# Conv 0 of an S4D block: VectorE's order fixed from the last doublings to the second norm, its spectra in four tiles, and the constants for U loaded twice

## The chip, the cores and the metric

The kernel runs on one core of one Trainium2 chip. A core has five engines with a queue each: TensorE (PE, with its weight loads PEld), VectorE (DVE), ScalarE (ACT), GpSimd (POOL) and SyncE (SP, which only issues DMAs). Each engine works through its own list of instructions in the order in which the program put them there, and waits on semaphores where an instruction needs something that another engine or a DMA has not finished. The metric is device time in microseconds (us) for one execution, the median of several runs.

## The reference

An adaLN-conditioned block on x of shape (1, 2048, 576), all float32: a layer norm with shift and scale, a long convolution whose kernel comes from an S4D state-space model with 128 states a channel, a gated residual, a second norm, and a dense ReLU layer 576 to 4608 to 576 with a gated residual.

```python
dt = exp(log_dt); A = -exp(log_A_real) + 1j * A_imag; C = (C_real + 1j * C_imag) * dt[:, None]
K = 2 * einsum("dn,dnl->dl", C, exp((A * dt[:, None])[:, :, None] * arange(L))).real
y = irfft(rfft(u_t, 2 * L) * rfft(K, 2 * L))[..., :L] + u * D_skip        # per channel
sa, ca, ga, sb, cb, gb = split(silu(c) @ w_mod, 6)
h = layernorm(x) * (1 + ca) + sa;  x = x + ga * conv(h)
h = layernorm(x) * (1 + cb) + sb;  x = x + gb * (relu(h @ w1) @ w2)
```

## The kernel before, in words

The 2048 positions are cut into four blocks of 512. Block s of the convolution needs kernel taps of blocks 0 to s, so the dense layer (FFN) of block 0 can start once block 0 has been convolved; everything of blocks 1 to 3 is then spread between the FFN's matmuls by `step`, which draws from generators. This study is about the front, which nothing covers: taps of block 0, convolution of block 0, second norm, first FFN matmul (`hps`).

**Taps of block 0** (`KGen.first`). The 576 channels come in six groups g of 96. `values` makes two factors by exp, sin and cos; `doubling` (L210) grows factor W1 from 1 to 16 powers in four steps, each two products `t`, `T` and two sums; in the last step the sums are POOL's. `multiply` has TensorE form the taps `kps`, `rows` copies them out into `ke`, and `store` (L346) writes them to DRAM as `kd`, one tile `kd_0_p` for each half p of the channels: groups 0 to 2 are half 0, groups 3 to 5 half 1. Factors W1, W2 and `zs` (in DRAM W1d, W2d, Zd) are kept for the later blocks; the stores of the last groups are put off (`held`).

**Conv 0** (`conv0`, L953). Each half p: `load_kt` reads the taps back as `kt`; VectorE adds the skip weights to it (`kt <- kt,dsk`, L974); `transform` is a first DFT stage on TensorE, with constants `fcU` for the signal h and `fcK` for the taps, 8 matmuls that ScalarE copies to SBUF as Z (ZU, ZK, Z1); VectorE's `butterfly1` (4 instructions, to W) and `butterfly2` (6, to the spectra U or K) finish it. `product` makes Y = K U (2 products, then 2 pairs of product T and sum), butterflies lead back to V, and `inverse` (TensorE, `ps_i`) brings the result, which VectorE adds to x2 (L899). For half 1 `transform1` does the taps' transform and first butterfly on TensorE (16 matmuls, 8 copies, to WK). `mod_late` computes the modulation rows sb, cb, gb: three weight tiles `wm`, one buffer, each loaded by POOL's queue after TensorE is done with the one before. `norm2` takes statistics (bn_stats, bn_aggr), a square root on ScalarE, the normalised h2, its transposes (`ps_t`), and splits the result in high and low parts xh, xl.

**What sets the order.** A scheduler orders each engine's instructions except those that `keep_in_program_order` holds; which one it puts first shows in the order of the built program. Memory is shared by pools: `late` (right side) holds the factor tiles, and when it closes, the FFN's pool `ff` takes its place, so that the FFN's first weights `r` cannot be loaded before the held stores of W1d and W2d have landed. The FFN splits each weight tile r into w and a low remainder (`split1`, L1084; `split2`, L1094 and L1095; for block 0 on VectorE). Pool `cvb` of the spectra (tiles X) opens late too.

Of the kernel before, what the change touches and what calls it, by code (L numbers as in the profile page):

```python
# [18 lines left out]
P = 128  # L19
L = 2048  # L20
D = 576
# [25 lines left out]
class KGen:  # L47
# [13 lines left out]
    def open(self, early, late):  # L61

        def pool(ctx, n, side, **kw):
            return ctx.enter_context(self.tc.tile_pool(name=n, bufs=1, side=side, **kw))

        self.pa, self.ss = pool(early, "kg_a", "left"), pool(early, "kg_s", "left", space=PSUM)
        self.pw, self.pc, self.pt = (pool(late, f"kg_{x}", "right") for x in "wct")
        self.ps, self.ph = (pool(late, f"kg_{x}", "right", space=PSUM) for x in ("ps", "ph"))
        self.Zp = self.ps.tile([P, 2, 8 * G], F32, name="Zp")
# [140 lines left out]
    def doubling(self, g):  # L210

        v, p = self.nc.vector.tensor_tensor, self.pool
# [38 lines left out]
    def first(self, setup, mod, norm):  # L251
# [26 lines left out]
        def values(g, then):  # L278
# [15 lines left out]
            for u in range(2):  # L294
                nc.sync.dma_start(out=k.Zd[2 * g + u], in_=zs[:, :, :, u * H : u * H + H])
# [32 lines left out]
        for g in (0, 2):  # L328
# [6 lines left out]
            values(g + 2, lambda: None)  # L335
            values(g + 3, lambda: rows(g))
# [3 lines left out]
        multiply(4)  # L340
        double(5)
# [5 lines left out]
    def store(self, s, p, ke, eng):  # L347

        for t in range(2):
# [3 lines left out]
            if s == 0:  # L353
                self.tc.keep_in_program_order(d)
# [100 lines left out]
class Body:  # L455
    def __init__(self, nc, tc, I, out):
        self.nc, self.tc, self.I, self.out = nc, tc, I, out

# [98 lines left out]
    def mod_late(self):  # L557

        nc, act = self.nc, self.nc.scalar.activation
        cb = self.cv.tile([P, 5, 32], F32, name="cb")  # L560
        nc.vector.tensor_copy(cb, self.ct.unsqueeze(2).broadcast_to([P, 5, 32]))
        for i, nm in ((3, "sb"), (4, "cb"), (5, "gb")):
            w = self.cv.tile([P, 5, D], F32, tag="wm", bufs=1, name=f"wm_{nm}")
# [12 lines left out]
            row = self.cv.tile([P, 2 * P], F32, tag="row", bufs=1, name=f"row_{nm}")  # L576
# [45 lines left out]
    def main(self, ctx, kg, first, late):  # L622
# [3 lines left out]
        for t, n in ((self.fcU, "fcu"), (self.fcK, "fck"), (self.gc, "gc")):  # L626
            nc.sync.dma_start(out=t, in_=I[n])
        self.ended = -1
        with ExitStack() as c:
            self.conv0(ctx, c, first, late)  # L630
# [29 lines left out]
        self.ffn([block0(), block1(), block2(), self.finish(2)])  # L660
# [7 lines left out]
    def half(self, name):  # L668
        return self.cv.tile([P, 4, PC], F32, tag="T", bufs=2, name=name)
# [25 lines left out]
    def butterfly1(self, Z, W):  # L695
        v = self.nc.vector.tensor_tensor
# [5 lines left out]
    def butterfly2(self, W, X, sgn):  # L702
        v = self.nc.vector.tensor_tensor
# [25 lines left out]
    def stats(self, src, st):  # L729

        for i in range(4):
            self.nc.vector.bn_stats(out=st[i], in_=src(i))  # L732
# [133 lines left out]
    def product(self, Y, Ka, Ua, first):  # L866

        v = self.nc.vector.tensor_tensor
# [18 lines left out]
    def inverse(self, x2, p, ops):  # L887

        xv = x2.rearrange("m n (dd p q) -> m n dd p q", dd=4, p=2)
        for n2 in (0, 2, 1, 3):  # L890
# [8 lines left out]
            self.nc.vector.tensor_tensor(xv[:, n2, :, p], pv, xv[:, n2, :, p], op=ALU.add)  # L899
            yield 0.45  # L900

    def norm2(self, s, x2, xp):
# [28 lines left out]
        for kk in (4, 0, 1, 2, 3):  # L931
# [11 lines left out]
            nc.scalar.activation(hi, xf, AF.Copy)  # L943
            yield None
            if kk == 4:
                v(xs[64:P], xf[64:P], xs[64:P], op=ALU.subtract)
            else:
                v(xl[:, kk], xf, hi, op=ALU.subtract)  # L948
            yield 0.7

    def conv0(self, ctx, c, first, late):

        nc, I = self.nc, self.I  # L953
        v, kept = nc.vector.tensor_tensor, self.tc.keep_in_program_order
# [9 lines left out]
        self.cps, self.nps = self.pool(c, "cpsa", space=PSUM), 2  # L964
        fcKn, gcn = (cva.tile([P, 4, P], F32, name=n) for n in ("fcKn", "gcn"))
        kt = [self.load_kt(0, 0)]
        for t, a in zip((fcKn, gcn), I["neg"]):
            nc.sync.dma_start(out=t, in_=a)
        hv = self.h.rearrange("m n (dd p q) -> m n dd p q", dd=4, p=2)

        def src_K(p):
            ktv = kt[p].rearrange("p (t dd g) q -> p t dd g q", t=2, g=2)
            dv = self.dsk.rearrange("o (dd p q) -> o dd p q", dd=4, p=2)[:, :, p]
            v(ktv[0:1, 0, :, 0], ktv[0:1, 0, :, 0], dv, op=ALU.add)  # L974
# [10 lines left out]
        self.save(self.Ud[0][0], U0)  # L985
        W = S(3, "W")
# [9 lines left out]
        kept(nc.sync.dma_start(out=x2, in_=I["x"][0].rearrange("n m d -> m n d")))  # L996
        for dst, src in self.held:
            kept(nc.sync.dma_start(out=dst, in_=src))
# [3 lines left out]
        self.cv = cvb = self.pool(c, "cvb")  # L1002
        self.cps, self.nps = self.pool(c, "cpsb", space=PSUM, side="right"), 4

        def X(name):
            return cvb.tile([P, 4, 2, PC], F32, tag="X", name=name)

        Y = X("Y0")
        run(self.product(Y, K0, U0, True))
        V = S(3, "V0")  # L1010
        run(self.butterfly1(Y, V))
        W, U1 = X("W"), None
# [4 lines left out]
        mod = self.mod_late()  # L1017
# [12 lines left out]
        run(self.inverse(x2, 0, ops))  # L1030
        W = S(1, "WK")
        run(self.transform1(src_K(1), self.fcK, fcKn, W))
        K1 = S(0, "K1")
        run(self.butterfly2(W, K1, -1))
        self.save(self.Rd[0][1], K1)
        next(mod)
        Y = X("Y1")
        run(self.product(Y, K1, U1, True))
        W = S(3, "W")
        run(self.butterfly1(Y, W))  # L1040
        next(mod)
        V1 = S(1, "V1")
        run(self.butterfly2(W, V1, 1))
        run(self.inverse(x2, 1, lambda n2: [(g(n2, c), V1[:, n2, c]) for c in range(2)]))
        next(mod, None)
        run(self.norm2(0, x2, self.xp[0]))

# [268 lines left out]
```

## Time and profile before

| | us |
|---|---|
| median of 3 runs | 1449.44 (1447.53 to 1452.51) |
| profiled execution | 1447.2 |
| its span by the trace | 1445.4 |
| what lies around the span | 1.8 |

| busy over the span | us | share |
|---|---|---|
| PE | 1250.2 | 86% |
| DVE | 878.0 | 61% |
| ACT | 503.5 | 35% |
| POOL | 197.8 | 14% |

The profile has views that answer different questions. The busy time by stretches tells which engine is full where. The waits say who stood still for whom, in total. The timeline gives every instruction with its start, its length and, in brackets, how long its engine had idled before it and what ended that idle time. The DMA view gives the time from a DMA's issue to its landing. The granted clock (PEclk) is the share of full speed at which TensorE was allowed to run. Starts of instructions are counted from the span's start; a mean of an instruction includes some overlap with the next one, so that a run of equal instructions is read from start to start.

### The profile page before, as it was taken

How to read it: one execution, taken by the hardware profiler on the slowest of the kernel's cores; microseconds unless marked ns; L12 is line 12 of the kernel's file. 1: busy time of each engine (PE TensorE's matmuls, PEld its weight loads, DVE VectorE, ACT ScalarE, POOL GpSimd, SP SyncE). 2: the span in 40 equal slices, each digit the busy share in tenths (PEclk: the TensorE clock that was granted, in tenths of full speed). 3: DMA queues.
4: the chain of work that ended last, by engine and by line, in shares of the span. 5: the costliest groups of instructions: out<-in, count | busy, mean ns of one | idle time of the engine just before them, and what ended most of it. 6: DMA issues, size and time to landing. Idle time of an engine off the chain costs nothing. (4 is left out here: it accounts for less than half of the span.)

```text
span 1445.4 us, 25948 instructions
## 1 busy us (share of the span) xinstructions
PE 1250.2 (86%) x10600; PEld 981.7 (68%) x10600; DVE 878.0 (61%) x1353; ACT 503.5 (35%) x1007; POOL 197.8 (14%) x271
## 2 busy tenths in 40 slices
PE   5123757999988997788999999999999999999997
PEld 3123534777867775566777778777887878888885
DVE  5988657899756679837936789363899332110101
ACT  6984212322221340252234322633322253222221
POOL 2767202010111111011110110010100000000000
PEclk9555867999999998999999999999999999999998
DMA  6666496587698694759877998575989656666661
GB/s 184 229 231 214 139 323 228 180 287 245 210 370 308 207 329 169 246 163 392 285 252 262 322 319 294 159 256 149 374 308 338 199 163 205 194 194 197 189 187 59
DMA packets 135222, 345.31 MB, mean 239 GB/s; under 512 B 23424, under 2 KB 23712, under 8 KB 135104
## 3 DMA queue, kind: packets, MB, share of 16 engines
q1 hardware_dynamic: 107824, 220.52, 47.1%
q0 software_dynamic: 26992, 122.55, 23.4%
q8 instruction: 83, 1.36, 0.4%
q10 hardware_dynamic: 288, 0.59, 0.1%
q14 instruction: 35, 0.29, 0.1%
HBM read 262.22 MB, written 81.40 MB: 238 GB/s over the span
## 5 line engine op out<-in xcount | busy, mean ns | idle before, releaser
L1133 PE MATMUL acc<-hh,w 128*128 128x512 f32 x1296 | 422.0, 400 | 3.1 <-DVE w L1094 3.0
L1108 PE MATMUL hps<-xh,w 128*128 128x512 f32 x1152 | 399.9, 407 | 0.0
L1114 DVE SCALAR_TENSOR_TENSOR hl<-hps,hh 128x512 fp32r<-128x512 f32 x144 | 99.5, 691 | 324.0 <-ACT hh L1113 323.7
L1133 PEld LDWEIGHTS acc<-hh,w 128*128 128x128 f32 x1296 | 242.7, 189 | 57.3 <-DVE w L1094 3.4
L1133 PE MATMUL acc<-hl,w 128*128 128x512 f32 x720 | 281.1, 401 | 0.1
L1108 PEld LDWEIGHTS hps<-xh,w 128*128 128x128 f32 x1152 | 219.3, 191 | 50.4 <-ACT xh L943 1.2
L1108 PE MATMUL hps<-xl,w 128*128 128x512 f32 x576 | 234.4, 407 | 0.5 <-DVE xl L948 0.5
L1113 ACT ACTIVATE hh<-hps 128x512 fp32r<-128x512 f32 x144 | 86.1, 598 | 335.4 <-PE hps L1108 327.2
L1091 ACT ACTIVATE w<-r 128x576 fp32r<-128x576 f32 x144 | 98.8, 686 | 276.1 <-PE acc L1133 218.1
L1133 PEld LDWEIGHTS acc<-hl,w 128*128 128x128 f32 x720 | 136.0, 189 | 29.9 <-DVE hl L1114 0.5
L1108 PEld LDWEIGHTS hps<-xl,w 128*128 128x128 f32 x576 | 109.8, 191 | 26.9 <-DVE xl L948 2.0
L1082 ACT ACTIVATE w<-r 128x640 fp32r<-128x640 f32 x144 | 105.4, 732 | 57.6 <-DMA L1d<-w 35.2
L1108 PE MATMUL hps<-xs,w 128*128 128x512 f32 x288 | 104.1, 427 | 19.0 <-DVE hl L1114 7.4
L243 PE MATMUL kps<-W,W 128*32 128x16 f32 x2304 | 39.4, 217 | 81.4 <-POOL W L59 55.4
L243 PEld LDWEIGHTS kps<-W,W 128*32 128x32 f32 x2304 | 37.3, 151 | 84.4 <-POOL W L59 56.2
L411 PEld LDWEIGHTS kps<-W1r,W2r 128*32 128x32 f32 x3456 | 67.8, 146 | 37.5 <-issue 23.2
L411 PE MATMUL kps<-W1r,W2r 128*32 128x48 f32 (+2 forms) x3456 | 76.6, 238 | 14.2 <-issue 8.0
L884 DVE TENSOR_TENSOR Y<-Y,T 128x1152 f32<-128x1152 f32 x64 | 84.9, 1355 | 0.1
L1108 PEld LDWEIGHTS hps<-xs,w 128*128 128x128 f32 x288 | 54.6, 192 | 34.8 <-issue 7.8
L1234 POOL DMA_DIRECT2D out_dram<-x x16 | 8.8, 548 | 479.2 <-DVE x L1232 479.2
L687 ACT ACTIVATE Z<-ps_f 128x288 f32<-128x288 f32 x104 | 42.4, 408 | 65.3 <-PE ps_f L686 65.2
L686 PE MATMUL ps_f<-h,fcU 128*128 128x288 f32 x128 | 47.2, 471 | 14.1 <-DVE W L235 14.0
(209 smaller groups left out, 1444.7 us busy)
## 6 DMA issues: line engine op xcount, KB each, us to landing
r<-in_w_dram SPq DMA_DIRECT2D x144, 320.0 KB, 3.9
r<-in_w_dram SPq DMA_DIRECT2D x144, 288.0 KB, 3.7
w<-L1d SPq DMA_DIRECT2D x108, 320.0 KB, 3.0
w<-L2d SPq DMA_DIRECT2D x108, 288.0 KB, 3.3
W2r<-W2d POOLq DMA_DIRECT2D x18, 1536.0 KB, 9.8
W2d<-W SPq DMA_DIRECT2D x12, 1536.0 KB, 7.7
Ua<-Ud POOLq DMA_DIRECT2D x15, 1152.0 KB, 10.6
W<-W1d POOLq DMA_DIRECT2D x18, 768.0 KB, 8.7
```

Of the source, the lines that this page charges most:

```text
L243: self.nc.tensor.matmul(ps[32 * dd : 32 * dd + 32, 12 * u + q, :], W2[:, r, :, ch], W1[:, u, :, r, ch], start=(r == 0), stop=(r == 1),)
L411: nc.tensor.matmul(ps[32 * dd : 32 * dd + 32, q, :], W2[:, r, :, ch], W1[:, :, r, ch], start=(r == 0), stop=(r == 1),)
L686: nc.tensor.matmul(o, fc[:, n2, c, :], src(n2), start=True, stop=True)
L687: nc.scalar.activation(Z[:, n2, c], ps[:, :PC], AF.Copy)
L884: v(y, y, T, op=op or ALU.add)
L1082: nc.scalar.activation(w[:, 0], r, AF.Copy)
L1091: nc.scalar.activation(w[:, 0:D], r, AF.Copy)
L1108: nc.tensor.matmul(ps, a, x, start=(i == 0), stop=(i == 13))
L1113: nc.scalar.activation(hh, ps, AF.Relu)
L1114: nc.vector.scalar_tensor_tensor(hl, ps, 0.0, hh, op0=ALU.max, op1=ALU.subtract)
L1133: nc.tensor.matmul(acc[i], a, x, start=(f == 0 and j in (0, 3, 6, 9, 12)), stop=(f == NF - 1 and j in (2, 5, 8, 11, 13)),)
L1234: nc.gpsimd.dma_start(out=ov[:, n2], in_=x2[:, n2])
```

## The change

Work in conv 0 is put in another order; no arithmetic is added or removed.

- `Body.kept` and `Body.v` chain instructions of one engine while `pinned` is set, from the start of `conv0` to its end: VectorE's tensor_tensor of the last two doublings, of conv 0, of the weight splits, bn_stats, and SP's loads and stores. ScalarE, TensorE and POOL are left to the scheduler.
- `early` is a second copy of the constants fcU and fcK, in a slot of the W1 tiles, loaded while groups 4 and 5 are made; ZU and ZK use it. fcU, fcK, gc and their negatives are loaded after the taps of half 0.
- Zd of group 5 is held too; the held W2d and Zd stores go out right after the load of `kt` 0, the held W1d stores after x2.
- The spectra of conv 0 live in four tiles S0 to S3 of the left pool (no X tiles); T uses slots of `kt`. The temporaries' pool (`kg_t`, and the PSUM of `kg_ps`) closes right after double(5), and the first `mod_late` load follows there.
- Product Y0 and its first butterfly come ahead of the load of `kt` 1. The first weight splits of the FFN, for g = 0 (both) and g = 1 (the first), come between the two inverse transforms; those of w2 for g = 1 and 2 come after the last xl.

```diff
     def doubling(self, g):
-        v, p = self.nc.vector.tensor_tensor, self.pool
+        v, p = self.k.v if g > NG - 3 else self.nc.vector.tensor_tensor, self.pool
...
             values(g + 2, lambda: None)
+            if g == 2:
+                t = k.early = self.pc.tile([P, 2, 4, 2, P], F32, tag="W1", bufs=3, name="early")
+                for i, n in enumerate(("fcu", "fck")):
+                    nc.sync.dma_start(out=t[:, i], in_=k.I[n])
             values(g + 3, lambda: rows(g))
...
         double(4)
         multiply(4)
+        yield
         double(5)
...
+    def kept(self, op):
+        if self.pinned:
+            e = op.ins.engine
+            if e in self.last:
+                self.tc.add_manual_dep(
...
+            self.last[e] = op.ins
+        return op
+
+    def v(self, *args, **kw):
+        return self.kept(self.nc.vector.tensor_tensor(*args, **kw))
...
+        early = self.early
         kt = [self.load_kt(0, 0)]
+        stores()
+        for t, n in ((self.fcU, "fcu"), (self.fcK, "fck"), (self.gc, "gc")):
+            load(t, I[n])
...
-        run(self.transform(lambda n2: hv[:, n2, :, 0], self.fcU, ZU))
-        run(self.transform(src_K(0), self.fcK, ZK))
+        run(self.transform(lambda n2: hv[:, n2, :, 0], early[:, 0], ZU))
         next(first)
+        run(self.transform(src_K(0), early[:, 1], ZK))
+        next(first)
+        kg.factors.close()
...
         self.save(self.Rd[0][0], K0)
+        Y = S(2, "Y0")
+        run(self.product(Y, K0, U0, True))
+        V = S(3, "V0")
+        run(self.butterfly1(Y, V))
         next(first, None)
         kt.append(self.load_kt(0, 1))
+        self.cps, self.nps = self.pool(c, "cpsb", space=PSUM), 4
         Z1 = S(2, "Z1")
...
         late.close()
         self.ff = self.pool(ctx, "ff", side="right")
+        next(self.start)
...
+        WK = S(1, "WK")
+        run(self.transform1(src_K(1), self.fcK, fcKn, WK))
         next(mod)
...
         V1 = S(1, "V1")
         run(self.butterfly2(W, V1, 1))
+        run(self.inverse(x2, 0, ops))
+        self.cv = self.pool(c, "cvb")
+        next(self.start)
         run(self.inverse(x2, 1, lambda n2: [(g(n2, c), V1[:, n2, c]) for c in range(2)]))
         next(mod, None)
         run(self.norm2(0, x2, self.xp[0]))
```

How the order moves at three places. First VectorE in the middle of conv 0, before: `kt_2484` are the taps of half 1, Y0 and V0 belong to half 0, `w1_2887` is the FFN's first weight tile, and the row after the last one is the first butterfly of Z1.

```order
L974 TENSOR_TENSOR kt_2484<-kt_2484,dsk_205 1x4x72
L878 TENSOR_TENSOR Y0_2536<-K0_2279,U0_2266 128x4x288 x2
L882 TENSOR_TENSOR T_2539<-K0_2279,U0_2266 128x1152
L882 TENSOR_TENSOR T_2542<-K0_2279,U0_2266 128x1152
L884 TENSOR_TENSOR Y0_2536<-Y0_2536,T_2539 128x4x288
L884 TENSOR_TENSOR Y0_2536<-Y0_2536,T_2542 128x4x288
L561 COPY cb_2563<-ct_260 128x160
L698 TENSOR_TENSOR V0_2545<-Y0_2536 128x576
L699 TENSOR_TENSOR V0_2545<-Y0_2536 128x576
L698 TENSOR_TENSOR V0_2545<-Y0_2536 128x576
L699 TENSOR_TENSOR V0_2545<-Y0_2536 128x576
L1084 TENSOR_TENSOR w1_2887<-r1_2881,w1_2887 128x640
```

The same place now (L485 is the line of the new helper `v`; `kt_2513` are the taps of half 1):

```order
L485 TENSOR_TENSOR Y0_2302<-K0_2294,U0_2273 128x4x288 x2
L485 TENSOR_TENSOR T_2305<-K0_2294,U0_2273 128x1152
L485 TENSOR_TENSOR Y0_2302<-Y0_2302,T_2305 128x4x288
L485 TENSOR_TENSOR T_2308<-K0_2294,U0_2273 128x1152
L485 TENSOR_TENSOR Y0_2302<-Y0_2302,T_2308 128x4x288
L485 TENSOR_TENSOR V0_2311<-Y0_2302 128x576 x4
L485 TENSOR_TENSOR W_2601<-Z1_2518 128x576 x4
L485 TENSOR_TENSOR U1_2606<-W_2601 128x576 x2
L485 TENSOR_TENSOR U1_2606<-W_2601 128x288 x4
L485 TENSOR_TENSOR kt_2513<-kt_2513,dsk_205 1x4x72
L485 TENSOR_TENSOR K1_2685<-WK_2614 128x576 x2
```

The add to the taps of half 1 has moved from ahead of Y0 to behind U1, where K1 follows it directly, and the FFN's split has left this place (it now stands behind V1 and the four x2 adds of the first inverse).

Second, SP's queue at the end of the doublings, before: `kt_1941` are the taps of half 0.

```order
L276 DMA W2d_9_74<-W2_9_1802 128x4x768
L295 DMA Zd_8_97<-zs_4_1847 512x1x48
L295 DMA Zd_9_98<-zs_4_1847 512x1x48
L350 DMA kd_0_0_57<-ke_0_1212 64x1152 x2
L295 DMA Zd_10_99<-zs_5_1907 512x1x48
L295 DMA Zd_11_100<-zs_5_1907 512x1x48
L627 DMA fcU_1927<-in_fcu_dram 128x1024
L627 DMA fcK_1928<-in_fck_dram 128x1024
L627 DMA gc_1929<-in_gc_dram 128x1024
L1051 DMA kt_1941<-kd_0_0_57 128x16x72
```

And now (the first half of `early` stands two rows further up, ahead of W2d_8):

```order
L279 DMA W2d_9_74<-W2_9_1802 128x4x768
L279 DMA Zd_8_97<-zs_4_1847 512x1x48
L279 DMA Zd_9_98<-zs_4_1847 512x1x48
L342 DMA early_1860<-in_fck_dram 128x1024
L358 DMA kd_0_0_57<-ke_0_1212 64x1152 x2
L1102 DMA kt_1939<-kd_0_0_57 128x16x72
L1003 DMA W2d_10_75<-W2_10_1863 128x4x768
L1003 DMA W2d_11_76<-W2_11_1864 128x4x768
```

The load of `kt` 0 has moved ahead of three constants and of Zd 10 and 11, one constant has come ahead of the `kd` stores, and the two W2d stores now follow the load instead of the load of x2.

Third, ScalarE at the second norm, before: `mv` are the four square roots, `row_gb` and `m_gb` belong to the third modulation row.

```order
L583 ACTIVATE m_cb_214<-mpt_cb_2715 128x5
L742 ACT_TABLE_LOAD
L742 ACTIVATE mv_2794<-mv_2794,eps_201 128x1
L742 ACTIVATE mv_2797<-mv_2797,eps_201 128x1
L742 ACTIVATE mv_2800<-mv_2800,eps_201 128x1
L742 ACTIVATE mv_2803<-mv_2803,eps_201 128x1
L577 ACTIVATE row_gb_2771<-mps_gb_2745 128x128
```

And now:

```order
L1145 ACTIVATE w2_2745<-r2_2596 128x576
L606 ACTIVATE row_gb_2793<-mps_gb_2767 128x128
L608 ACTIVATE row_gb_2793<-mps_gb_2767 32x64 x2
L612 ACTIVATE m_gb_215<-mpt_gb_2797 128x5
L775 ACT_TABLE_LOAD
L775 ACTIVATE mv_2816<-mv_2816,eps_201 128x1
```

The third modulation row has moved ahead of the table load and the square roots. From the first FFN instruction that needs the norm (`hh`, `hl`, `hps`) to the end, PE, DVE, ACT and POOL have the same instructions in the same order before and now; SP's differ in the order of the first few.

More of the change, by code (lines that the diff above doesn't have):

```diff
@@ L625, in main @@
         self.fcU, self.fcK, self.gc = (sm.tile([P, 4, 2, P], F32, name=n) for n in ("fcU", "fcK", "gc"))
[L626 to L627 removed]
         self.ended = -1
+        self.gens = []
+        self.start = self.ffn(self.gens)
         with ExitStack() as c:
[L630 removed]
+            self.conv0(ctx, c, kg, first, late)
         self.nps = 1
@@ L1054, in load_kt @@
         )
+        if s == 0:
+            self.kept(d)
         return kt
```

123 lines of the change are left out of this document (73 added, 50 removed).

## The prediction, made before the run

> **What bounds the kernel now.** I first split the time at the first FFN matmul. The busy time by stretches: start and end of the stretch, its length, then busy time of PE, PEld, DVE, ACT and POOL with counts, the granted clock, the DMA share and GB/s.
>
> ```profile
> 135.70:258.10 122.40, 74.36 (x1073) 52.66 (x1073) 78.19 (x147) 26.29 (x67) 24.43 (x30) 0.73 0.69 235
> 258.10:440.00 181.90, 172.13 (x2093) 135.63 (x2093) 150.52 (x165) 47.41 (x81) 20.67 (x32) 0.99 0.74 257
> 800.00:1445.00 645.00, 629.40 (x2745) 505.77 (x2743) 293.31 (x411) 214.08 (x364) 30.88 (x44) 0.99 0.71 229
> ```
>
> After 258.1 TensorE is busy 95% and more: the FFN fills it. The 122.4 us before, from the start of the last doublings, hold VectorE's chain doubling, butterflies, product, butterflies, norm; nothing else is full there, and VectorE itself is busy only 78.19 us. It idles 44.2, and the waits of VectorE between 135 and 259 say for whom (waiter, waited for, total, times, longest):
>
> ```profile
> DVE kt L974 <- DMA kt<-kd: 16.1, 1, 16.1
> DVE w L1084 <- ACT w L1082: 11.5, 1, 11.5
> DVE x L899 <- PE ps_i L894: 4.3, 3, 3.7
> DVE w L1094 <- ACT w L1091: 4.0, 1, 4.0
> DVE W L698 <- ACT ZU L687: 3.1, 1, 3.1
> DVE K L710 <- ACT WK L726: 0.6, 1, 0.6
> ```
>
> The rest, some 5 us, lies in the last doublings and the norm and stays. Where the first two stand, the timeline of that stretch shows, with who held the awaited thing up:
>
> ```profile
> 170.44 0.46 DVE L712 TENSOR_TENSOR K<-W 128x288 f32<-128x288 f32 x1
> 178.14 0.31 PEld L243 LDWEIGHTS kps<-W,W 128*32 128x32 f32 x6 [2.78 <-issue]
> 182.80 0.38 SPq L1051 DMA_DIRECT2D kt<-kd  x1
> 185.90 0.39 SPq L996 DMA_DIRECT2D x<-in_x_dram  x1
> 186.99 0.45 DVE L974 TENSOR_TENSOR kt<-kt,dsk 1x288 f32<-1x288 f32 x1 [16.10 <-DMA kt<-kd]
> 187.37 2.61 DVE L878 TENSOR_TENSOR Y<-K,U 128x1152 f32<-128x1152 f32 x2
> 208.69 1.51 ACT L1082 ACTIVATE w<-r 128x640 fp32r<-128x640 f32 x2 [22.37 <-DMA r<-in_w_dram]
> 209.46 0.82 DVE L1084 TENSOR_TENSOR w<-r,w 128x640 fp32r<-128x640 f32 x1 [11.52 <-ACT w L1082]
> ```
>
> K is done at 170.9 and Y0 needs nothing else, but the add to the taps of half 1 stands ahead of it; these come from DRAM after `multiply(5)` ends at 178.5. Later the butterfly of Z1 stands behind a weight split whose tile arrives at 208.7. Both are order, not work.
>
> **The change part by part.** I make the sum on the stretch of 122.4 us.
>
> *Gone.* The four waits of 16.1, 11.5, 4.0 and 0.6, since Y0, V0 and the butterflies now precede what waited, and 3.1 for ZU, whose constant is now loaded early: 35.3 us. What is late next in their place follows below. The two later w2 splits move behind the norm, under the first FFN matmuls: 2 x 0.7 = 1.4, by these rows (216.78 to 217.51 is one split):
>
> ```profile
> 216.78 0.22 DVE L1094 TENSOR_TENSOR w<-r,w 128x64 fp32r<-128x64 f32 x1
> 216.91 0.69 DVE L1095 TENSOR_TENSOR w<-r,w 128x512 fp32r<-128x512 f32 x1
> 217.51 0.46 DVE L899 TENSOR_TENSOR x<-ps_i,x 128x288 f32<-128x288 f32 x1
> ```
>
> Of the 4.3 us for the inverse I take 0.7 to stay (0 to 4.3), because four x2 adds and the three splits (4 x 0.46, 2 x 0.82 and 0.7, some 4 us) now stand between V1 and the last adds, time in which TensorE makes the second inverse: 3.6 saved. Together 40.3.
>
> *New wait 1, taps of half 0.* Their add now stands between the two last doublings, so all of VectorE's queue is behind it.
>
> ```profile
> 143.27 0.38 SPq L1051 DMA_DIRECT2D kt<-kd  x1
> 145.11 0.35 DVE L231 TENSOR_TENSOR t<-W,Zp 128x192 f32<-128x192 f32 x1
> kt<-kd SPq DMA_DIRECT2D x1, 576.0 KB, 7.8
> ...
> kt<-kd SPq DMA_DIRECT2D x1, 576.0 KB, 4.2
> W2d<-W SPq DMA_DIRECT2D x1, 1536.0 KB, 5.5
> ```
>
> The first doubling ends at 145.1. The load was issued at 143.3 and took 7.8 us behind three constants; the one of half 1, alone, took 4.2. Now those constants are behind it, but one of 512 KB is ahead of `kd`: a third of W2d's 5.5 us, 1.8. Issue 143.3 to 145.1, landing 147.5 to 152.9, so a wait of 2.4 to 7.8. The issue also loses five rows ahead of it, so I take 3.3, near the low end. The copy of two constants costs nothing else: VectorE and TensorE don't see it.
>
> *New wait 2, Z1.* Its tile is Y0's, so its copies start only after V0; TensorE can have four banks ready. In the old order the eight took this long:
>
> ```profile
> 178.49 7.38 PE L686 MATMUL ps_f<-h,fcU 128*128 128x288 f32 x16
> 184.65 0.90 ACT L687 ACTIVATE Z<-ps_f 128x288 f32<-128x288 f32 x2 [0.55 <-PE ps_f L686]
> ```
>
> The first butterflies need four copies, 4 x 0.45 = 1.8; for the second half TensorE still has four matmuls to make. From 1.8 to 5 (7.4 less the overlapped butterflies); I take 3.4.
>
> *New wait 3, the taps' transform of half 1.* It needs `kt` 1 with its add, which now comes after U1, and K1 follows with nothing in between. By order `multiply(5)` comes a little earlier than before and `kt` 1 lands 8.5 us after it (178.5 to 187.0), well before U1 ends: 145.1 + 3.3, 22.7 as before up to K0 (145.1 to 170.9 less 3.1), some 10.5 for Y0 and V0 (six at 1.3, four at 0.7), 3.4, and 5.5 for Z1's ten make some 190.5. The 16 matmuls are then bare:
>
> ```profile
> 220.56 1.17 PE L723 MATMUL ps_f<-kt,fcK 128*128 128x288 f32 x2
> 221.52 0.91 PE L725 MATMUL ps_f<-kt,fcKn 128*128 128x288 f32 x2
> 223.24 0.65 PE L723 MATMUL ps_f<-kt,fcK 128*128 128x288 f32 x2
> 223.73 0.65 PE L725 MATMUL ps_f<-kt,fcKn 128*128 128x288 f32 x2
> 218.00:224.00 6.00, 6.00 (x18) 4.30 (x18) 2.00 (x5) 1.68 (x5) 0.00 (x0) 0.66 1.01 355
> 224.00:230.00 6.00, 4.97 (x62) 3.34 (x60) 5.28 (x9) 2.21 (x9) 1.71 (x3) 1.00 0.70 260
> ```
>
> From start to start 0.96 us each, then 0.49: the granted clock doubles near 222. So 7 to 15 us; I take 8, full speed, since TensorE will just have done `multiply(5)`, Z1 and the first modulation row. The Trainium skill ("TensorE: Matmul & The Clock Gate", Part 1) says that the clock is full after about 3.4 us of sustained work and halves after an idle window as long; by it, an estimate, the 16 matmuls would cost 7.7 if no gap precedes and 9.5 after one, and the sum would move by 2 at most. The rows here are slower: TensorE had worked since 216.6, over 5 us, when the clock rose, so the upper end stays with the rival below.
>
> *New wait 4, the square root.*
>
> ```profile
> 248.50 2.22 PE L572 MATMUL mps_gb<-wm_gb,cb 128*32 128x128 f32 x50
> 243.94 1.28 ACT L742 ACT_TABLE_LOAD   x1
> 250.75 0.67 ACT L742 ACTIVATE mv<-mv,eps 128x1 f32<-128x1 f32 x3 [3.33 <-DVE mv L741]
> L732 DVE BATCH_NORM_STATS2 st<-x 128x6 f32<-128x288 f32 x8 | 3.2, 450 | 0.1
> ```
>
> Before, the table was loaded early and the roots came ahead of the third modulation row. Now the row's products (2.2, at half clock up to twice that) run after the last inverse; with its copies and the 1.28 us table load it stands ahead of the roots, while VectorE's statistics need 3.2 and a little. 0 to 4; I take 2.
>
> *Nothing.* W1 of group 5 now waits for `multiply(3)` instead of `multiply(2)`; VectorE idles there for ScalarE's sine anyway. The port beside POOL:
>
> ```profile
> 157.55 4.96 POOL L59 TENSOR_TENSOR W<-T,T 128x384 f32<-128x384 f32 x4 [10.15 <-issue]
> 160.05 1.58 DVE L699 TENSOR_TENSOR W<-ZU 128x576 f32<-128x576 f32 x1
> 166.53 0.75 DVE L698 TENSOR_TENSOR W<-ZK 128x576 f32<-128x576 f32 x1
> ```
>
> Butterflies beside POOL's sums take 1.58 instead of 0.75, some 2 us in all, and the new order has the same neighbours; cost 0. The Trainium skill ("SBUF — State Buffer", Two separate sides) calls the pair of ports an exclusive lock: the later of the two fully blocks. By that rule, an estimate, the butterflies would stand still for most of POOL's 4 us, 2 more than before, and the sum would be 22; the trace shows half of it.
>
> *Sum.* New waits 3.3 + 3.4 + 8 + 2 = 16.7; gain 40.3 - 16.7 = 23.6, with the ends of all four (11.2 to 31.8) and of the inverse between 5 and 30. From the first FFN matmul on the order is the same, so this passes on whole: 1447.2 - 23.6 = 1423.6 for a profiled execution. The median of the runs lies 2.2 above that execution, so 1426.
>
> **The rivals.**
> 1. *The waits come back.* TensorE idles before the taps' transform and before the inverse and works there at half clock, or the second modulation weights, loaded only after the first row, hold up TensorE's queue ahead of the inverse. For it: the clock of 0.73 in the stretch. Wait 3 becomes 12 to 15 and the inverse's 4.3 stays: 8 to 11 less, gain 13 to 16, 1433 to 1436; with a late `kt` 0 too, 1441.
> 2. *Absorbed by the FFN.* If transfers, not TensorE, bound block 0 after 258, an earlier start would only wait: 1449. Against it: the DMA share is 0.74 there, and all those transfers are issued by the FFN's own progress.
> 3. *Slower: the fixed order stalls on the FFN's weights.* The three splits now stand ahead of the last x2 adds, whatever else is ready. Their tiles come behind x2 and the four held W1d stores; before, that took from 185.9 to 208.7, 22.8 us. x2 is issued after Z1's transform, at some 186, so they land near 209, 7 us ahead of need (190.5 + 8, 16 for K1, Y1 and V1, and 1.8 of adds: 216). Each us beyond costs one; it decides from 24 us of lateness, landing after 240. With 30 us late: 1449.4 + 6 = 1455.
> 4. *The order isn't what the change says.* The built order shows it; no chance of its own.
>
> **How the numbers follow.** About 0.3% (4 us) is what this measurement can tell from no change. Forecast, gain 18 to 30: 0.64. Rival 1, gain 5 to 18: 0.20. Gain over 30: 0.05. Rival 2: 0.05. Rival 3: 0.06. Faster 0.89, same 0.05, slower 0.06. The range runs from the gain of 30 with the 3 us by which runs of before vary, 1417, to rival 1's far end, 1441.
>
> **What would show it.** Right: no wait of VectorE for `kt` of half 1 over 1 us and none for the weight splits; one of 2 to 8 at the taps of half 0, some 8 for WK, 2 to 5 for Z1; first FFN matmul near 234; the 1187 us from there to the end unchanged within 3. Wrong: a wait over 5 us at a split (rival 3), 12 and more for WK with the clock at 0.5 (rival 1), or an earlier first matmul with a longer rest (rival 2).

## The result, and the profile after

| | median us | profiled execution | its span |
|---|---|---|---|
| before | 1448.49 (1445.54 to 1452.51, 4 runs) | 1447.2 | 1445.4 |
| changed | 1429.64 (1423.64 to 1432.92, 4 runs) | 1428.99 | 1427.2 |

The ratio is 0.9863, 95% interval 0.9822 to 0.9905: faster, 3.6 us above the forecast of 1426. First the stretch that the sum was made on, from the start of the last doublings to the first FFN matmul, in the busy times of the changed kernel (columns as before). It was 122.4 us and is 99.03; VectorE is busy 77.56 of it, nearly as before, and idles 21.5 instead of 44.2:

```profile
138.57:237.60 99.03, 67.67 (x1069) 49.63 (x1068) 77.56 (x142) 24.72 (x64) 24.37 (x30) 0.76 0.81 288
```

VectorE's waits in it (waiter, waited for, total, times, longest). Of the five large ones of before four are gone, and that for the inverse (`ps_i`) is 1.7 instead of 4.3; one of the forecast new ones, WK, is now the largest:

```profile
DVE K L485 <- ACT WK L759: 9.1, 1, 9.1
DVE W L485 <- ACT Z L720: 2.6, 2, 2.0
DVE kt L485 <- DMA kt<-kd: 2.2, 1, 2.2
DVE xf L972 <- PE ps_t L967: 2.0, 1, 2.0
DVE x L485 <- PE ps_i L927: 1.7, 3, 0.6
DVE mv L780 <- ACT mv L775: 1.2, 1, 1.2
DVE xs L979 <- ACT xs L976: 1.0, 1, 1.0
DVE W L485 <- ACT ZK L720: 0.9, 1, 0.9
```

Where they stand, in the timeline of VectorE:

```profile
138.57 0.35 DVE L485 TENSOR_TENSOR t<-W,Zp 128x192 f32<-128x192 f32 x1
...
150.32 0.45 DVE L485 TENSOR_TENSOR kt<-kt,dsk 1x288 f32<-1x288 f32 x1 [2.19 <-DMA kt<-kd]
...
174.58 2.62 DVE L485 TENSOR_TENSOR Y<-K,U 128x1152 f32<-128x1152 f32 x2
...
193.58 0.44 DVE L485 TENSOR_TENSOR kt<-kt,dsk 1x288 f32<-1x288 f32 x1
203.08 2.90 DVE L485 TENSOR_TENSOR K<-WK 128x576 f32<-128x576 f32 x6 [9.07 <-ACT WK L759]
...
221.08 2.29 DVE L485 TENSOR_TENSOR w<-r,w 128x640 fp32r<-128x640 f32 x4
```

Y0 (174.58) follows K0 at once. The add to the taps of half 1 (193.58) and the FFN splits (221.08) no longer wait, but K1 stands still for 9.07 right behind the add.

The doublings start 2.8 us later than before (138.57, not 135.77). That arises in code which the change doesn't touch: TensorE's first 20 matmuls, before and after. They start 0.48 us apart, most of them, until about 17 us before and until 23 us after, and 0.24 from then on; the profile's record of the clock has its first entry, full clock, at 17.25 and at 22.98.

```profile
13.34 7.62 PE L555 MATMUL mps_ga<-wm_ga,cb 128*128 128x288 f32 x20 [13.34 <-DVE cb L550]
```

```profile
13.46 10.28 PE L583 MATMUL mps_ga<-wm_ga,cb 128*128 128x288 f32 x20 [13.46 <-DVE cb L578]
```

So the span's 18.2 are 23.3 gained in the stretch (122.3 less 99.0), 2.8 lost at the start, and 2.3 lost behind the first FFN matmul (1187.4 to 1189.6). The last two are looked at below.

### The profile page after: what moved, and what is told of

It is laid out like the page before. It is cut to its first block, busy times and chain, and to the rows that moved or that the text cites. A ratio compares the mean times of both kernels' runs of the same rounds, so it can differ in the third digit from the quotient of the medians.

```text
span 1427.2 us, 25955 instructions
## 1 busy us (share of the span) xinstructions
PE 1250.5 (88%) x10600; PEld 983.3 (69%) x10600; DVE 878.8 (62%) x1353; ACT 503.1 (35%) x1007; POOL 197.7 (14%) x271
## 5 line engine op out<-in xcount | busy, mean ns | idle before, releaser
L246 PE MATMUL kps<-W,W 128*32 128x16 f32 x2304 | 40.0, 218 | 89.1 <-POOL W L59 56.1
L485 DVE TENSOR_TENSOR Y<-Y,T 128x1152 f32<-128x1152 f32 x64 | 84.7, 1349 | 0.2
L485 DVE TENSOR_TENSOR w<-r,w 128x512 fp32r<-128x512 f32 (+2 forms) x108 | 57.8, 570 | 31.9 <-ACT w L1145 20.4
```

Source lines behind the costliest of these rows:

```text
L246: self.nc.tensor.matmul(ps[32 * dd : 32 * dd + 32, 12 * u + q, :], W2[:, r, :, ch], W1[:, u, :, r, ch], start=(r == 0), stop=(r == 1),)
L485: return self.kept(self.nc.vector.tensor_tensor(*args, **kw))
```

## The experiments

Theory: the gain is VectorE's standstill for data that its next work didn't need; a wait counts only as far as nothing covers it, and what is won at the first FFN matmul reaches the end. Rivals: the early constants and the memory did it; the fixing only confirms an order that comes anyway; waits add up one for one. The table has for each kernel its profile cut at three starts (`t <- W,Zp` of the last doublings, `K <- WK`, the first `hps`). The rows come from several comparisons, in which the kernel before had medians from 1448.5 to 1450.6, so that a few us between the medians of two rows say little.

| kernel | median us (runs) | ratio to the kernel before, 95% | doublings to K1 | K1 to first FFN matmul | from there on |
|---|---|---|---|---|---|
| before | 1448.49 (4) | 1 | 89.1 | 33.2 | 1187.4 |
| before_again | 1448.81 (1) | | 87.7 | 33.5 | 1189.7 |
| changed | 1429.64 (4) | 0.9863 (0.9822 to 0.9905) | 64.5 | 34.5 | 1189.6 |
| after_again | 1430.36 (6) | 0.9868 (0.9844 to 0.9891) | 65.2 | 34.7 | 1190.1 |
| u_kt1 | 1439.41 (10) | 0.9940 (0.9918 to 0.9961) | 76.7 | 32.4 | 1188.3 |
| u_split | 1452.00 (10) | 1.0006 (0.9982 to 1.0030) | 88.1 | 35.1 | 1186.3 |
| u_early | 1433.39 (4) | 0.9878 (0.9847 to 0.9909) | 66.7 | 35.3 | 1193.5 |
| u_pin | 1441.41 (8) | 0.9937 (0.9916 to 0.9958) | 79.2 | 33.3 | 1195.3 |
| x_w2d | 1437.92 (4) | 0.9923 (0.9896 to 0.9950) | 62.2 | 38.4 | 1194.6 |
| i_add | 1425.32 (4) | 0.9836 (0.9799 to 0.9873) | 61.1 | 34.1 | 1192.3 |
| i_kt0 | 1431.79 (4) | 0.9888 (0.9855 to 0.9921) | 67.3 | 35.2 | 1190.0 |
| i_gb | 1433.96 (4) | 0.9892 (0.9866 to 0.9919) | 64.4 | 38.3 | 1193.4 |
| i_root | 1428.89 (6) | 0.9850 (0.9825 to 0.9876) | 64.2 | 33.3 | 1191.1 |
| best | 1421.12 (4) | 0.9805 (0.9779 to 0.9831) | 61.8 | 32.7 | 1189.8 |

**u_kt1: the first of the four waits put back.**

```diff
+        next(first, None)
+        kt.append(self.load_kt(0, 1))
+        taps1 = src_K(1)
         Y = S(2, "Y0")
...
-        next(first, None)
-        kt.append(self.load_kt(0, 1))
...
-        run(self.transform1(src_K(1), self.fcK, fcKn, WK))
+        run(self.transform1(taps1, self.fcK, fcKn, WK))
```

> The changed kernel, with one step undone: the add to the taps of half 1 stands ahead of product Y0 again (T and the taps share three slots instead of two, so that the old place is possible). My theory: the gain came from VectorE's queue no longer standing still for data that the next instructions don't need, and what a wait costs is what is left of it after what it covers. Y0 would start when the taps of half 1 land, at 191 instead of 174.6, 16.5 us later; Z1's copies follow V0, the taps' transform follows Z1 on TensorE and ends near 216, so that most of its 9.1 us disappears behind Z1 and U1: K1 some 12 us later than 203, the time 10 to 14 us longer, near 1441. Rival A, waits add up one for one: 16 us longer, 1446. Rival B, the gain came from the early constants and the pools, and the place of the add doesn't matter: within 3 us of the changed kernel.

VectorE's timeline in that kernel:

```profile
185.97 0.45 DVE L485 TENSOR_TENSOR kt<-kt,dsk 1x288 f32<-1x288 f32 x1 [13.33 <-DMA kt<-kd]
...
212.85 2.90 DVE L485 TENSOR_TENSOR K<-WK 128x576 f32<-128x576 f32 x6 [6.15 <-ACT WK L759]
```

The wait of 13.3 is back; that for WK shrinks only to 6.2, since Z1 moved back with it. K1 comes 12.2 us later (76.7 against 64.5), as worked out; the median is 9.8 above the changed kernel's, just under the 10 to 14 expected. Rival B falls, and waits don't add up one for one.

**u_split: the second wait put back.**

```diff
         split1(0)
+        yield
         split2(0)
...
+        next(self.start)
         W = S(0, "W")
         run(self.butterfly1(Z1, W))
```

> The changed kernel, with one step undone: VectorE's first split of an FFN weight stands ahead of Z1's first butterfly again. My theory: the tile r of that split lands near 212 whatever VectorE does, since it stands behind the held stores, so Z1's butterfly starts at about 214 instead of 187.3, and all that follows it, the add to the taps of half 1 and their transform too, moves by the same: some 25 us longer, 1453 to 1457, slower than the kernel before. Rival A, a wait put back costs what it cost in the kernel before: 11.5 us longer, 1441. Rival B, it is hidden, as TensorE's taps' transform can cover it: under 3 us.

VectorE's timeline, the split:

```profile
207.08 0.82 DVE L485 TENSOR_TENSOR w<-r,w 128x640 fp32r<-128x640 f32 x1 [24.01 <-ACT w L1137]
```

One misplaced split costs 23.5 us up to K1 and 22.4 in the median: the whole gain, and not the 11.5 for which the same wait stood before. It is a little under the 25 and the 1453 to 1457 expected, since the tile came at 206.3 and not at 212; that it would be slower than the kernel before did not show. Before, the wait was short because the tile came at about the same time (208.7) and VectorE had already lost 16.1 to the other wait. A wait in the profile is what is left behind the waits ahead of it.

**u_early: without the second copy of the constants.**

```diff
-            if g == 2:
-                t = k.early = self.pc.tile([P, 2, 4, 2, P], F32, tag="W1", bufs=3, name="early")
...
+        for t, n in ((self.fcU, "fcu"), (self.fcK, "fck"), (self.gc, "gc")):
+            load(t, I[n])
         kt = [self.load_kt(0, 0)]
         stores()
```

> The changed kernel without the second copy of the constants: fcU, fcK and gc are loaded ahead of the taps of half 0, as in the kernel before, and ZU and ZK use them. My theory: fcU lands at 147 to 149, ZU's transform on TensorE ends 5 to 7 us later than 147.5, multiply of groups 4 and 5 and the taps' transform ZK stand behind it, and the taps of half 0 land some 2 to 3 us later too; VectorE then waits for ZK instead, and for WK: 4 to 8 us longer, 1434 to 1438. Rival A, the terms of the prediction, ZU's 3.1 and 3.6 for three constants ahead of the taps: 6.7, but seen as a wait for ZU of some 3 and one for the taps of half 0 near 5.8. Rival B, it is covered by the doublings: under 2 us.

TensorE's timeline from ZU's transform through `multiply` of group 4 (the doublings start at 135.3 here):

```profile
143.14 6.24 PE L715 MATMUL ps_f<-h,fcU 128*128 128x288 f32 x16 [9.68 <-DVE T L481]
...
155.91 2.11 PE L246 MATMUL kps<-W,W 128*32 128x16 f32 x127 [4.24 <-issue]
159.56 2.11 PE L246 MATMUL kps<-W,W 128*32 128x16 f32 x117 [1.54 <-issue]
```

K1 comes 2.2 us later, the median is 3.8 higher, with intervals that overlap: under the theory's range, over rival B's. ZU's transform did end 5 us later (14.1 after the start of the doublings; 9.0 in the changed kernel), but `multiply` behind it ended only 1.1 later, because its second pause took 1.54 instead of 4.27. VectorE never waits for ZU, so rival A's sum names the wrong place. The pauses come up again in x_w2d. VectorE's timeline at K1:

```profile
201.98 2.90 DVE L481 TENSOR_TENSOR K<-WK 128x576 f32<-128x576 f32 x6 [10.57 <-ACT WK L755]
```

Up to the add to the taps of half 1 only 0.6 us were lost; the other 1.5 are this wait, 10.6 instead of 9.1, because six pairs of the taps' transform ran at half speed there and three in the changed kernel. So the early constants are worth about 0.6 in these profiles, and the rest of the difference is the clock's.

**u_pin: the order not fixed.**

```diff
-        self.pinned = True
+        self.pinned = False
```

> The changed kernel, with pools, tiles, early constants and code order as they are, but without the chains that fix VectorE's and SP's order, so that the scheduler chooses. In its order ScalarE has the three FFN splits ahead of the copies of WK and VectorE has its splits ahead of K1, and x2 is loaded behind three weight tiles. My theory: the copies of WK wait for the last of these weight tiles, which lands near 215, K1 starts near 220 instead of 203: 12 to 20 us longer, 1441 to 1450, so that nearly all of the gain is gone. Rival: the gain came from the other parts (memory, early constants, code order), and the chains only confirm an order that comes anyway: within 3 us.

ScalarE's timeline in that kernel, a weight split and the copy of the first late modulation row (`row_sb`) behind it:

```profile
205.19 0.74 ACT L1136 ACTIVATE w<-r 128x640 fp32r<-128x640 f32 x1 [4.15 <-DMA r<-in_w_dram]
205.83 0.26 ACT L606 ACTIVATE row_sb<-mps_sb 128x128 f32<-128x128 f32 x1
```

TensorE's, the transpose of that row and the taps' transform behind it:

```profile
206.14 0.48 PE L610 MATMUL mpt_sb<-ident,row_sb 128*128 128x128 f32 x1 [11.55 <-ACT row_sb L606]
206.41 1.24 PE L756 MATMUL ps_f<-kt,fcK 128*128 128x288 f32 x2
```

And VectorE's, at K1:

```profile
215.61 3.14 DVE L485 TENSOR_TENSOR K<-WK 128x288 f32<-128x288 f32 x6 [6.28 <-ACT WK L759]
```

The theory had the copies of WK behind a split that waits for its tile. In the trace it is the copy of the modulation row that stands there; TensorE waits 11.6 for it, and the taps' transform behind it starts 14.4 us later than in the changed kernel, counted from the doublings. Some 6 of these would have been lost anyway, as VectorE, in the scheduler's order, made the add to these taps that much later. K1 comes 14.7 us later, the median is 11.8 above the changed kernel's, just under the 12 to 20 expected. Fixing the order is most of the change; memory, constants and code order alone leave 8 us of 19 (1449.59 less 1441.41 in its comparison).

**x_w2d: two held stores back to their old place**, to see what TensorE's pauses in `multiply` are.

```diff
         kt = [self.load_kt(0, 0)]
-        stores()
```

> The changed kernel, with one step undone: the held stores of W2d and Zd go out behind the load of x2 again, not right behind the load of the taps of half 0. It asks why multiply of groups 4 and 5 has pauses without a wait on TensorE: 4.48, 4.27, 1.76 and 4.04 us in the changed kernel, where the kernel before had 1.17, 1.64, 2.33 and 2.67. Theory: TensorE's own instructions come late while other transfers are queued (the changed kernel has W2d, Zd and constants in flight from 146.6 to 165.4). Without them the first two pauses fall to 1 to 2.5, multiply of group 4 ends some 4 us earlier and the wait for ZK (0.9) goes; nothing else is gained, since the add to the taps of half 1 stays behind U1; in exchange the FFN's first weight tiles land some 9 us later, near 226 instead of 217, and the splits, due at 221, wait 4 to 6 us for them: 2 to 6 us longer in all, 1432 to 1436. Rival: the pauses belong to the instruction stream itself; they stay within 0.5 us of 4.48 and 4.27, and only the loss at the splits is seen.

The two pauses of `multiply` of group 4 as stretches of busy time (last columns: clock, DMA share, GB/s), in the changed kernel:

```profile
150.83:155.31 4.48, 0.01 (x1) 0.00 (x1) 4.31 (x13) 0.00 (x0) 0.00 (x0) 0.71 1.03 410
157.46:161.73 4.27, 0.00 (x2) 0.00 (x1) 4.27 (x6) 0.00 (x0) 3.00 (x3) 0.50 1.04 383
```

The first such pause in the kernel before:

```profile
163.85:165.02 1.17, 0.00 (x0) 0.00 (x1) 1.17 (x3) 0.00 (x0) 0.00 (x0) 1.00 0.00 0
```

Both in this kernel, where constants are in flight only up to the first:

```profile
151.57:155.29 3.72, 0.00 (x1) 0.00 (x1) 3.62 (x10) 0.00 (x0) 0.00 (x0) 0.50 0.30 111
157.41:158.94 1.53, 0.00 (x1) 0.00 (x0) 1.53 (x3) 0.00 (x0) 1.50 (x2) 0.50 0.00 0
```

With the DMA engines full these pauses are over 4 us, with nothing on them 1.2 to 1.5; u_early has 4.24 (share 1.00) and 1.54 (0.00). The first one here fell only to 3.72, not to the 1 to 2.5 expected: transfers still filled the DMA engines for its first 1 us. The DMA view has the reason, a block of instructions on its way (queue, packets, MB, share of time). The changed kernel, inside its first pause:

```profile
q1 hardware_dynamic: 606, 1.81, 100.7%
q8 instruction: 1, 0.02, 1.4%
```

The kernel before, in the 3.84 us of matmuls ahead of its pause:

```profile
q8 instruction: 1, 0.02, 2.1%
```

There the block had come before TensorE stopped; in the changed kernel it came 2 us into the pause, behind the other transfers. So the theory holds for the pauses. But the share over the pause doesn't decide; what counts is when the block lands. In best, a block that had come just before a pause left it at 1.30 with a share of 0.96. The changed kernel's last pause in `multiply(5)` was long with a share of 0.30:

```profile
178.20:182.24 4.04, 0.00 (x0) 0.00 (x0) 3.97 (x4) 0.00 (x0) 0.00 (x0) 0.50 0.30 111
```

Its block landed 2.6 us into it, behind the store of K0 (`Rd <- K`, 1152 KB). The price of the move shows in VectorE's timeline:

```profile
224.56 0.82 DVE L485 TENSOR_TENSOR w<-r,w 128x640 fp32r<-128x640 f32 x1 [4.94 <-ACT w L1135]
```

A split waited 4.9, as expected. K1 came 2.3 us earlier and the first FFN matmul 1.7 later than in the changed kernel, counted from the doublings. The median, 8.3 above the changed kernel's, is more than the 2 to 6 expected: the doublings also started 3.0 us later, as W1 of group 5 waited 5.1 for `multiply(3)`, and the end took 4.9 longer, which the spread of that part covers.

**i_add: the add to the taps of half 1 ahead of U1.**

```diff
+        taps1 = src_K(1)
         U1 = S(2, "U1")
         run(self.butterfly2(W, U1, -1))
...
-        run(self.transform1(src_K(1), self.fcK, fcKn, WK))
+        run(self.transform1(taps1, self.fcK, fcKn, WK))
```

> The changed kernel, with the add to the taps of half 1 between the first and the second butterflies of Z1 instead of behind U1. The taps land at 190.6, when the first butterflies end (190.7). My theory: the 9.1 us for WK are the taps' transform laid bare, from the add on; with the add 2.8 us earlier, and TensorE without its 2.2 us of idleness ahead of the transform (its first six matmuls then ran at half speed), K1 starts 3 to 4.5 us earlier, and the time is 3 to 4.5 us shorter, near 1426. Rival A, the transform is bound by what stands ahead of it on TensorE (first modulation row, until 191.9), and stays slow: 1 to 2.5 us. Rival B, the add now waits for taps that land later than in that profile, and U1 behind it waits too: no change or slower.

The taps' transform in TensorE's timeline of the changed kernel:

```profile
194.12 1.30 PE L756 MATMUL ps_f<-kt,fcK 128*128 128x288 f32 x2 [2.21 <-DVE kt L485]
195.21 1.17 PE L758 MATMUL ps_f<-kt,fcK 128*128 128x288 f32 x2
196.17 1.10 PE L756 MATMUL ps_f<-kt,fcK 128*128 128x288 f32 x2
197.10 0.65 PE L758 MATMUL ps_f<-kt,fcKn 128*128 128x288 f32 x2
197.59 0.65 PE L756 MATMUL ps_f<-kt,fcK 128*128 128x288 f32 x2
```

And in this one:

```profile
188.76 0.72 PE L756 MATMUL ps_f<-kt,fcK 128*128 128x288 f32 x2
...
190.18 0.65 PE L756 MATMUL ps_f<-kt,fcK 128*128 128x288 f32 x2
190.66 0.65 PE L758 MATMUL ps_f<-kt,fcKn 128*128 128x288 f32 x2
```

Without the idle 2.21 there are no slow pairs (about 1 us from start to start; 0.49 at full speed): K1 3.5 us earlier, the wait 5.6 instead of 9.1. Of the 3.5, 2.4 come from the earlier start and 1 from the speed. The median is 4.3 shorter, with intervals that overlap. The profile bears the theory out, except that idleness doesn't always bring the slow pairs. In i_root below TensorE idled 2.18 at this place, and ran at full speed:

```profile
194.71 0.72 PE L756 MATMUL ps_f<-kt,fcK 128*128 128x288 f32 x2 [2.18 <-DVE kt L485]
195.27 0.65 PE L758 MATMUL ps_f<-kt,fcK 128*128 128x288 f32 x2
```

**i_kt0: the wait for the taps of half 0 removed.**

```diff
+            if g == NG - 1 and i == 2:
+                self.k.taps0()
...
-        run(self.transform(src_K(0), early[:, 1], ZK))
+        ks = []
+        self.taps0 = lambda: ks.append(src_K(0))
         next(first)
+        run(self.transform(ks[0], early[:, 1], ZK))
```

> The changed kernel, with the add to the taps of half 0 two steps into the last doubling instead of ahead of it, so that VectorE doesn't wait 2.2 us for these taps. My theory: nothing is gained by it, since ZK, the next thing that VectorE needs from these taps, is set by TensorE (multiply of group 4, with its pauses, until 163.8, then ZK's transform until 169.8): the wait for ZK grows from 0.9 to about 3, and the time stays within 1.5 us of the changed kernel's. Rival, the wait counts one for one, as the prediction's sum took it: 2.2 us shorter.

VectorE's longest waits there, from 133 us on:

```profile
DVE K L487 <- ACT WK L761: 10.4, 1, 10.4
DVE W L487 <- ACT Z L722: 3.8, 2, 2.4
DVE W L487 <- ACT ZK L722: 3.4, 2, 2.3
```

The 2.2 are gone and come back at once at ZK (3.4 instead of 0.9). That nothing is gained holds; K1 was even 2.2 to 2.8 later than in the two profiles of the changed kernel, outside the 1.5 allowed: Z1's matmuls (8.4 us of them, 6.2 there) and the first of WK's ran slow.

**i_gb: the third modulation row ahead of the second inverse.**

```diff
+        next(mod, None)
         run(self.inverse(x2, 1, lambda n2: [(g(n2, c), V1[:, n2, c]) for c in range(2)]))
-        next(mod, None)
```

> The changed kernel, with the third modulation row's products ahead of the second inverse on TensorE instead of behind it (its weights are there, and TensorE idles 4.7 us ahead of that inverse). My theory: the 1.2 us that VectorE waits for the square root go, since row and table load are then done early, and the second inverse starts on a TensorE that has just worked, so that some of the 1.7 us at the last x2 adds goes too: 1 to 2.5 us shorter. Rival: the row delays the inverse by as much, no change.

TensorE's timeline, the row's products and what they waited for:

```profile
217.74 3.86 PE L601 MATMUL mps_gb<-wm_gb,cb 128*32 128x128 f32 x50 [5.50 <-DVE x L485]
```

A miss: the first FFN matmul comes 3.8 us later, counted from K1, where it was expected 1 to 2.5 earlier. The row's PSUM bank is one that the first inverse holds until VectorE has added it to x2, so it doesn't fill the idle time but starts after it, at half speed, and pushes the second inverse back (wait 6.4 instead of 1.7).

**i_root: the row's copies behind the square roots**, TensorE's order kept.

```diff
+            self.root = sq.ins
...
-        next(mod, None)
-        run(self.norm2(0, x2, self.xp[0]))
+        tail = self.norm2(0, x2, self.xp[0])
+        for w in tail:
+            if w == 2.0:
+                break
+        with self.tc.issue_after(self.root):
+            next(mod, None)
+        run(tail)
```

> The changed kernel, with ScalarE's copies of the third modulation row behind the square roots instead of ahead of table load and roots; TensorE's order stays. It measures the prediction's new wait 4 by itself. My theory: the table load then runs while VectorE still makes its statistics, the wait of 1.2 us for the root goes, and TensorE's transposes for the norm start 1 us earlier: 0.9 to 1.3 us earlier at the first FFN matmul, counted from the start of the first modulation row's second part; by the median hardly to be told from the changed kernel (0 to 3 us shorter). Rival: the row's transpose, which now stands behind these copies on TensorE and ahead of the norm's transposes, takes the wait's place: no change at the first FFN matmul.

ScalarE's timeline:

```profile
217.99 1.28 ACT L775 ACT_TABLE_LOAD   x1
228.61 0.85 ACT L775 ACTIVATE mv<-mv,eps 128x1 f32<-128x1 f32 x4 [9.34 <-DVE mv L774]
```

The table is now loaded 10 us before the roots, and the wait for them is gone. From K1 to the first FFN matmul 33.3 instead of 34.5 and 34.7; in the median it can't be told from the changed kernel. Counted as the expectation did, the first FFN matmul comes 1.6 and 2.3 earlier, more than the 0.9 to 1.3, because the taps' transform ran at full speed here (wait for WK 7.6).

**best: the two diffs of i_add and i_root together.**

> The changed kernel with both the add to the taps of half 1 ahead of Z1's second butterflies and the third modulation row's copies behind the square roots. Theory: the two savings lie at different places of VectorE's chain and add up: 3.5 to 4.5 and about 1.2, some 5 us shorter than the changed kernel, 1423 to 1426, and the wait for WK 5 to 6 us instead of 9.1. Rival: with K1 earlier, the FFN splits stand ahead of weight tiles that land only at 212 to 217, and a wait for these takes back what is gained beyond 4 us: 1425 to 1427, with a wait at a split.

No wait stands at a split; the one for WK is 5.6. From the doublings to the first FFN matmul it takes 94.5 instead of 99.0 and 99.9, and the median is 1421.12 against 1430.36 for the changed kernel beside it, with intervals that don't overlap. The profile accounts for 5 of these 9 us; how much of the rest is chance is open. It is the fastest of all, 28 us below the kernel before in the same comparison (1449.11).

**after_again and before_again: nothing altered.**

> The changed kernel once more, unaltered, to see what in its first profile was chance. There, TensorE's first 20 matmuls (first modulation row, from 13.5) took 10.28 us, where ten other profiles of this study, with the same instructions up to there, took 7.3 to 8.1; and from the first FFN matmul to the end it took 1189.6, where these took 1186.3 to 1195.3. If the 2.8 us at the start are chance (theory): 7.3 to 8.1 again, the first FFN matmul at 234 to 236 instead of 237.6, the rest within 1186 to 1195, median within 3 us of 1429.6. If they belong to the change (rival): 10.3 again, and 237 to 238.

> The kernel before once more, unaltered, for a second look at what follows the first FFN matmul: 1187.4 us in its first profile, 1189.6 and 1190.1 in two profiles of the changed kernel. If some 2 us of the front's gain are given back later (theory A): 1186.3 to 1188 again. If the rest is only as scattered as in the other kernels of this study, 1186.3 to 1195.3 with the same instructions (theory B): any value in there, as well above 1189 as below. The stretch from the start of the last doublings to the first FFN matmul should again be 122 to 123 us, and the way there, from the second part of the first modulation row, 114.8 to 115.

The first 20 matmuls took 7.9 us this time (7.92 from 13.40), the first FFN matmul came at 235.9. So the 2.8 were chance, the chance of when the clock rises; i_root, whose first instructions are the same, had 10.05. Behind the first FFN matmul the kernel before took 1189.7 the second time, as the changed kernel: theory B, no sign of a gain given back beyond the 2 us by which these profiles scatter. Its front took 121.3, a little under the 122 to 123 expected. What makes the part behind the first FFN matmul differ by up to 9 us between kernels whose TensorE has the same matmuls there in the same order was not found.

## Why the prediction was right, point by point

| term, us | forecast | measured |
|---|---|---|
| waits gone: taps of half 1, w split, w2 split, ZU, K | 35.3 | 35.3 |
| two w2 splits behind the norm (measured: all that VectorE is busy less) | 1.4 | 0.6 |
| inverse, 4.3 to | 0.7 | 1.7 |
| new: taps of half 0 | 3.3 | 2.2 |
| new: Z1 | 3.4 | 2.6 |
| new: WK bare | 8 | 9.1 |
| new: square root | 2 | 1.2 |
| not forecast: ZK | 0 | 0.9 |
| sum, with what is left in the norm | 23.6 | 23.3 |

- The sum holds, and so do its parts, none off by more than 1.1. That it is right to 0.3 is partly luck: eight deviations of about 1 us, four each way, cancel. The first FFN matmul stood at 237.6, not 234, by the chance 2.8 at the start; at 235.9 the second time.
- **Taps of half 0** were put at 3.3 by the range's low end, and came out just under it (2.4), since the load took 4.2 from issue to landing, no more than the one of half 1 alone. But i_kt0 shows that the term was no loss in itself: ZK, bound by TensorE, would have taken its place. Here the prediction priced a wait by its length and not by what was late next.
- **WK** was 1.1 over the 8, by the clock: the taps' transform starts right behind the add (194.12) on a TensorE that had idled 2.21 for it, and its first three pairs take 1.5 us more than at full speed. That is a small piece of rival 1; "full speed" was the wrong choice, though i_root shows that it can happen.
- **`multiply(5)`** was to come "a little earlier than before". That was wrong: its last matmuls came 43.7 us after the doublings' start instead of 42.4 (182.24 and 178.15 in TensorE's timeline), because TensorE's own instructions came late behind the stores and constants moved behind the taps' load, and behind K0's store. It cost nothing at WK, as the add to the taps of half 1 didn't wait. The delay varies: with the same stores in place it was 39.2 in best and 43.6 in after_again.
- **Port beside POOL, cost 0**: VectorE's four butterflies of ZU took 4.8 us in all, 4.1 before; ZK's 2.8 instead of 3.8. That held; a full standstill, the rule of the Trainium skill ("SBUF — State Buffer", Two separate sides), did not show.
- **W1 of group 5, cost 0**: it waits 2.7 us, and the doublings start 114.9 after the second part of the first modulation row as before. It has no slack, though: in x_w2d and best, where `multiply(3)` paused longer, they started 3.0 and 1.9 later.
- **Rival 3** (stall on the FFN's weights) stayed off, with 3 us to spare and not the 7 worked out: the last tile's copy ran at 217.2 and the splits at 221.1. x_w2d shows the stall once the tiles come later.
- **Rival 2** (absorbed by the FFN): refuted; the first FFN matmul came 20.5 us earlier in the first pair of profiles and 21.5 in the second, and the median is some 19 shorter.

## What to carry to other kernels

Where an engine waits in a fixed order, ask of each wait what the engine could have done instead and what is late next: the same misplaced split stood as a wait of 11.5 us behind another wait and cost 23.5 alone, and removing 2.2 us at the taps of half 0 gained nothing. A transfer moved into a quiet stretch isn't free if another engine runs many small instructions there.

## What the runs showed of the hardware

- In `multiply`, TensorE stops after 128 or so of the small matmuls where the next 16 KB of its instructions are late. The 14 profiles have 196 such pauses of 0.9 us and more, up to 4.8, in the first 200 us, and each ended 1.0 to 1.6 us after such a block had landed. Before the 48 of over 2.6 us, the DMA engines had been busy 75% and more in the 2 us ahead of the block; before the 57 of under 1.5 us, mostly not at all (median 1%). The Trainium skill ("Runtime: NRT & Kernel Launch", Instruction fetch mechanics) gives the same block, 256 instructions, and calls the fetch hidden; here it isn't.
- After some small transposes and 2.21 us of idleness TensorE ran at half speed (194.12 to 197.10, granted clock 0.51); in i_root, after 2.18, it didn't (194.71 to 197.00, 1.00). The idle window that the Trainium skill states ("TensorE: Matmul & The Clock Gate", Part 1) is longer, about 3.4 us.
- The first 20 matmuls of a run took anything from 7.3 to 10.3 us, as the change from 0.48 to 0.24 us between their starts came 3 to 9.5 us after the first. That shifts all that follows.
